# Block products for the feed-forward of the last two batches, behind attention

## The chip, the cores and the metric

The kernel runs on one core of one Trainium2 chip. The time is device time of one execution in microseconds (us); three runs of the kernel before took 323.27, 323.76 and 324.39 us. The engines are PE (TensorE matmul; its weight loads are shown as PEld), VectorE (DVE), ScalarE (ACT), GpSimd (POOL, which only issues loads here) and SyncE (SP, which issues the stores of the output and the transposing copies of q and k).

## What is computed

Attention over 8 batches, 12 heads, 448 positions, 64 columns per head, with an extra term in the denominator, then a feed-forward over 3584 tokens of 768 columns, with a maximum over three up projections. In float32 in and out:

```python
scores = scale * np.matmul(q, k.transpose(0, 1, 3, 2))
e = np.exp(scores - m)
attn = e / (np.sum(e, axis=-1, keepdims=True) + np.exp(-m) + 1e-09)
x = np.matmul(attn, v)                                  # heads side by side: (3584, 768)
h = np.maximum(np.maximum(x @ w1, x @ w2), x @ w3)      # each (768, 768)
out = h @ w_out                                         # (768, 768)
```

## The kernel before

All matmul operands are float16 in SBUF; sums are float32 in PSUM. Attention is worked in 24 groups of four heads (3 groups make a batch). For one group, `visit` makes seven score tiles (one per 64 keys, line 276), each into a pair of PSUM banks; ScalarE turns each into `eT` with one exponential over 128x896 (line 299); `sum_e` on VectorE adds the seven up in `eS` (line 308); `den_group` multiplies `eS` with ones (line 322), and ScalarE takes the logarithm (line 341) and the exponential of its negative (line 348), which is the reciprocal `rb`; `num_group` makes the seven matmul steps of e times v (`av`, line 322) into another pair of banks, and two `norm_group` on VectorE multiply by `rb` and write `xT` (line 375), the transposed input of the feed-forward.

The feed-forward of a batch is cut in pieces. An up piece is a 128-row block of h for one batch and one of the three weights: six matmul steps of 448 columns. VectorE copies it to `hT` (line 497) or takes the maximum with what is there (line 499). An out piece is 128 output rows by 384 columns (`nh` is 0 or 1): six steps of 384 columns; VectorE scales it to float32 in `o_sb` (line 542), and a row tile of 128 x 768 goes out by two stores of 192 KB each on SP's queue (line 560). `o_sb` has six buffers. A pair of batches has 36 up pieces and 14 out pieces.

The order of PE's work is written by hand. From 73 us on, a "step" is one contraction step of a piece, made of four 64x64 matmuls, two for each half of the contraction rows (`step` and `half_step`; the matmul is line 758). `ORDER` (line 827) lists a group's operations, U (score tile), D (den) and N (av), each with a weight; after each operation `steps_for` puts in a share of feed-forward steps, by that weight over the sum of 38.9. `batch_done` adds a finished batch's pieces and sets `rate`, the steps per group. The four last out pieces of each batch are held back and come first with the next batch's out pieces. Pieces rotate over four PSUM banks (`ring_bank`); score, den and av tiles take two pairs of banks in turn (`double`), one pair at a time. Before that, a first stretch to 73 us has attention of the first groups and full-array feed-forward pieces (lines 510 and 533).

When attention is over, the remaining pieces run one after the other: before the change this is the feed-forward of the last batch and what is left of the one before.

Engines work through their instructions in order. So a matmul whose bank is not free, or whose input is not ready, holds every later matmul.

Of the kernel before, what the change touches and what calls it, by code (L numbers as in the profile page):

```python
# [10 lines left out]
FP32 = mybir.dt.float32  # L11
FP16 = mybir.dt.float16
AF = mybir.ActivationFunctionType
ALU = mybir.AluOpType
# [4 lines left out]
EDIV = 8.0  # L19
# [3 lines left out]
def kernel(  # L23
# [33 lines left out]
    )  # L57

    cpool = ctx.enter_context(tc.tile_pool(name="const", bufs=1))
    ld_pool = ctx.enter_context(tc.tile_pool(name="ld", bufs=5))  # L60
    p16_pool = ctx.enter_context(tc.tile_pool(name="p16", bufs=3))
    att_pool = ctx.enter_context(tc.tile_pool(name="att", bufs=4))
    e_pool = ctx.enter_context(tc.tile_pool(name="e", bufs=3))
    small = ctx.enter_context(tc.tile_pool(name="small", bufs=2))
    xt_pool = ctx.enter_context(tc.tile_pool(name="xt", bufs=2))
    ht_pool = ctx.enter_context(tc.tile_pool(name="ht", bufs=2))
    out_pool = ctx.enter_context(tc.tile_pool(name="outp", bufs=6))

    ps1 = ctx.enter_context(tc.tile_pool(name="ps1", bufs=2, space=bass.MemoryType.PSUM))
    ps2 = ctx.enter_context(tc.tile_pool(name="ps2", bufs=1, space=bass.MemoryType.PSUM))
    third = ExitStack()
    ps3 = third.enter_context(tc.tile_pool(name="ps3", bufs=1, space=bass.MemoryType.PSUM))
    turn = [0]
# [61 lines left out]
            reason="spreads the loads",  # L137
        )

    first_k = cpool.tile([128, 2, NJ, D], FP32, name="first_k")  # L140
    load_half(nc.sync, first_k, "k", 0, 0)
    load_half(nc.scalar, first_k, "k", 0, 1)
    load_group(0, "q")
# [22 lines left out]
                )  # L166
    w_sb = [cpool.tile([128, NDC, DFF], MMDT, name=f"w{i}") for i in range(4)]
    wout_sb = w_sb[3]


    def load_weight(i, f0=0, f1=DFF):
# [65 lines left out]


    def first_group():
        k16 = p16_pool.tile([128, NJ, 2, D], MMDT, tag="k16", name="k16", bufs=1)  # L240
        qkT = att_pool.tile([128, 2, NJ, 128], MMDT, tag="qkT", name="qkT")
        state[0] = {"qkT": qkT}
        cuts = (((0, 4), (0, 3)), ((4, NJ), (3, NJ)))
        for (k0, k1), _ in cuts:
            nc.vector.tensor_copy(
                out=k16[:, k0:k1].rearrange("p j s d -> p s j d"), in_=first_k[:, :, k0:k1]
            )
        for (k0, k1), (q0, q1) in cuts:
            nk = k1 - k0
            trT = single("trT", (NJ, 128), MMDT)  # L250
            for j in range(k0, k1):
                nc.tensor.transpose(
                    out=trT[:, j - k0, :], in_=k16[:, j].rearrange("p s d -> p (s d)"),
                    identity=ident16,
                )
            for j in range(q0, q1):
                transpose_slots(trT[:, nk + j - q0, :], raw[0]["q"][:, :, j])
            nc.vector.tensor_copy(out=qkT[:, 0, k0:k1], in_=trT[:, 0:nk])
            nc.vector.tensor_copy(out=qkT[:, 1, q0:q1], in_=trT[:, nk:NJ])
# [70 lines left out]
    def den_group(i):  # L330
        st = state[i]
        dps = double("den")
        av_tiles(
            [dps[:, r, 0:S] for r in range(2)],
            lambda r, c: ones16[half(r)],
            lambda r, c: st["eS"][half(r), c],
            True,
            True,
        )
        st["lnd"] = small.tile([128, 2, S], FP32, tag="lnd", name="lnd")  # L340
        nc.scalar.activation(  # L341
            out=st["lnd"], in_=dps[:, :, 0:S], func=AF.Ln, bias=1.0 / EDIV
        )

    def recip_group(i):
        st = state[i]
        st["rb"] = small.tile([128, 2, S], FP32, tag="rb", name="rb")
        nc.scalar.activation(  # L348
            out=st["rb"], in_=st.pop("lnd"), func=AF.Exp, bias=math.log(LAMBDA), scale=-1.0
        )  # L350

    def num_group(i, in_pair=True):
# [66 lines left out]
    def den_part(i, part):  # L419
        st = state[i]  # L420
        q0, q1 = PARTS[part]
        nq = (q1 - q0) * KC
        eT = st["eT", part]
        dps = double("den")
        terms = [eT[:, j] for j in range(NJ)]
        if "eP" in st:
            eP, n = st.pop("eP")
            terms = [eP[:, 0], eP[:, 1]] + terms[n:]
        for n, e in enumerate(terms):
            av_tiles(  # L430
                [dps[:, r, 0:nq] for r in range(2)],
                lambda r, c: ones16[half(r)],
                lambda r, c: e[half(r), c],
                n == 0,
                n == len(terms) - 1,
            )
        lnd = small.tile([128, 2, S], FP32, tag="lnd", name="lnd")
        nc.scalar.activation(
            out=lnd[:, :, 0:nq], in_=dps[:, :, 0:nq], func=AF.Ln, bias=1.0 / EDIV
        )  # L440
        rb = small.tile([128, 2, S], FP32, tag="rb", name="rb")
        nc.scalar.activation(
            out=rb[:, :, 0:nq], in_=lnd[:, :, 0:nq], func=AF.Exp, bias=math.log(LAMBDA), scale=-1.0
        )
        st["rb", part] = rb

# [80 lines left out]
    def out_piece(bp, t, nh, bank=None, done=False):  # L527
# [4 lines left out]
        for fc in range(0 if done else NFC):  # L532
# [6 lines left out]
            )  # L539
        last = bp == B // 2 - 1 and t == NT - 1  # L540
        cut = nh * NW + (NW // 2 if last and nh == NH - 1 else NW)
        nc.vector.tensor_scalar(  # L542
            out=o_sb[:, nh * NW : cut],
            in0=op_ps[:, 0 : cut - nh * NW],
            scalar1=1.0 / LAMBDA,
            scalar2=None,
            op0=ALU.mult,
        )
        if cut < nh * NW + NW:
            nc.scalar.activation(  # L550
                out=o_sb[:, cut:DM], in_=op_ps[:, NW // 2 : NW], func=AF.Copy, scale=1.0 / LAMBDA
# [153 lines left out]

    third.close()
    flush()
    single_pools.append(ctx.enter_context(tc.tile_pool(name="ps4", bufs=2, space=bass.MemoryType.PSUM)))
    pair_pools.pop()
    LAG = 2  # L710
    flow = []
# [64 lines left out]
    def left():  # L776
        return NDC * (len(pieces) + len(flow)) - count[0]
# [60 lines left out]
    TOTAL = sum(w for _, _, w in ORDER)  # L838


    def batch_done(b):
        add_ups(b)
        last_batch[0] = b == B - 1
        pieces.extend(held)
        held.clear()
        add_out(b, *((0, 3) if b % 2 == 0 else (3, 7)))
        if b < B - 1:
            held.extend(pieces[-HELD:])
            del pieces[-HELD:]
        rate[0] = (left() - (SPARE if b < B - 2 else LAST)) / 3  # L850

    SPARE, LAST = 30, 50
    rate = [0]
    batch_done(1)
    after(9, sum_e, MID, 1)
    after(14, sum_e, MID, 2)
# [3 lines left out]
    for i in range(MID, NI + 1):  # L860
        for op, j, w in ORDER if i > MID else ORDER[4:]:
            if op == "U" and i < NI:
                mm = visit([(i, j)])
                n, name = ((2, "v"), (3, "k"), (3, "q"), (0, ""))[j // 2]
                if n > 0 and i + n < NI and i > MID:
                    load_behind(mm, i + n, name, j % 2)
                steps[0] += 1
                if j == 2:
                    recip_group(i - 1)
                if j > 0:  # L870
                    after({1: 9, 2: 14, 3: 20, 4: 9, 5: 9, 6: 9}[j], sum_e, i, j)
                if j == (9 if i == 7 else 3) and PE_TR <= i + 2 < NI:
                    for n_ in range(2):
                        copy_qk(i + 2, n_)
                    dma_transpose(i + 2)
# [16 lines left out]
            steps_for(rate[0] * w / TOTAL if i < NI else (8 if op == "D" else 0))  # L892
    while late or left() or count[1] < count[0]:
        step()


# [28 lines left out]
```

## Time and profile before

| | |
|---|---|
| median of three runs | 323.76 us (323.27 to 324.39) |
| span of the profiled execution | 322.9 us, about 0.9 us below the median |
| PE busy | 308.2 us, 95% of the span |
| VectorE busy | 235.3 us, 73% |
| ScalarE busy | 191.7 us, 59% |
| last matmul ends | 317.45 us |
| share of the chain that ended last | PE 79%, DMA 14% |

The chain that ended last is followed back from the last instruction, at each step to what released it. It lies on loads until about 56 us and on PE after that. ScalarE's share is low because it has nothing to do after 274 us, when attention is over; in windows of 30 us before that it is 64 to 71% busy, and VectorE 79 to 80%. The mean of one instruction is its duration; instructions of one engine overlap a little, so that two 128x448 operations of VectorE start 0.53 us apart although each lasts 0.62.

### The profile page before, as it was taken

The numbers are of one execution on the slowest core, as the hardware profiler recorded it, in microseconds if no ns is written. First come the engines' busy times: TensorE is split into PE (matmuls) and PEld (weight loads), VectorE is DVE, ScalarE is ACT, GpSimd is POOL, SyncE is SP. The second block draws the span as 40 slices with busy tenths as digits, with TensorE's granted clock in tenths as the row PEclk, the third lists the DMA queues.
The fourth block names the chain that finished last, engine by engine and source line by source line (L and its number), as shares of the span: only waits on it lengthen the run. The fifth ranks groups of instructions, "written<-read, shape, count | busy, mean of one in ns | idle before, by whom it ended". The sixth has DMA issues, their size and how long they took to land.

```text
span 322.9 us, 14605 instructions
## 1 busy us (share of the span) xinstructions
PE 308.2 (95%) x6607; PEld 260.1 (81%) x6607; DVE 235.3 (73%) x443; ACT 191.7 (59%) x227; POOL 96.8 (30%) x166
## 2 busy tenths in 40 slices
PE   7669998999999999999999999999999999999993
PEld 6557676658998899988889877897787788887892
DVE  3446598998887878777769688878778777645652
ACT  2898859887786565575575685685576674000000
POOL 8947565840433132232222232232220000000000
PEclk9999999999999999999999999999999999999999
DMA  7999999999877975779969997899966500050046
GB/s 143 165 191 186 190 190 188 163 159 185 119 98 105 197 135 94 116 147 163 76 99 150 198 150 111 103 179 157 92 81 124 136 4 2 2 150 2 2 122 175
DMA packets 59517, 40.75 MB, mean 126 GB/s; under 512 B 32704, under 2 KB 56000, under 8 KB 59456
## 3 DMA queue, kind: packets, MB, share of 16 engines
q0 software_dynamic: 25344, 21.01, 48.1%
q1 hardware_dynamic: 33808, 18.39, 28.3%
q8 instruction: 51, 0.84, 1.1%
q10 hardware_dynamic: 304, 0.43, 0.5%
q14 instruction: 10, 0.08, 0.1%
HBM read 42.47 MB, written 11.01 MB: 166 GB/s over the span
## 4 chain that ended last, share of the span: by engine, by line
PE 79%; DMA 14%; POOL 3%; issue 1%; DVE 1%; ACT 0%; ACTq 0%; DVEq 0%; POOLq 0%
PE piece L758 59%; PE av L322 9%; PE stp L276 8%; DMA w<-in_moe_w_dram 7%; DMA ld_q<-in_q_dram 4%; DMA w<-in_moe_w_out_dram 2%; PE piece L533 2%; PE den L322 1%; PE piece L510 1%; DMA out_dram<-o_sb 1%; POOL w L180 1%; POOL w L181 1%; POOL ld_v L111 1%; POOL ld_q L111 1%; DVE eS L308 0%
## 5 line engine op out<-in xcount | busy, mean ns | idle before, releaser
L758 PE MATMUL piece<-xT,w 64*64 64x448 f16 x3024 | 177.7, 349 | 0.3 <-DVE xT L375 0.3
L299 ACT ACTIVATE eT<-stp 128x896 f16<-128x896 f32 x147 | 132.8, 916 | 65.9 <-PE stp L276 63.3
L758 PEld LDWEIGHTS <-w 64*64 64x64 f16 x3024 | 132.1, 107 | 21.2 <-issue 1.6
L276 PE MATMUL stp<-qkT 64*64 64x448 f16 (+2 forms) x756 | 71.3, 331 | 2.4 <-ACT eTp L394 0.8
L758 PE MATMUL piece<-w,hT 64*64 64x384 f16 x1224 | 68.3, 323 | 0.0
L308 DVE TENSOR_TENSOR eS<-eS,eT 128x896 f16<-128x896 f16 x105 | 65.0, 619 | 2.7 <-DVE eS L308 0.5
L499 DVE TENSOR_TENSOR hT<-hT,piece 128x448 f16<-128x448 f16 x84 | 51.9, 618 | 19.8 <-PE piece L758 16.8
L758 PEld LDWEIGHTS <-hT 64*64 64x64 f16 x1224 | 53.6, 107 | 4.4 <-issue 0.7
L111 POOL DMA_DIRECT2D ld_q<-in_q_dram x48 | 28.9, 606 | 60.3 <-PE piece L758 33.9
L111 POOL DMA_DIRECT2D ld_v<-in_v_dram x48 | 28.5, 599 | 47.7 <-PE stp L276 30.1
L276 PEld LDWEIGHTS <-qkT 64*64 64x64 f16 x756 | 32.1, 106 | 10.2 <-issue 5.5
L542 DVE TENSOR_SCALAR o_sb<-piece 128x384 f32<-128x384 f32 (+1 forms) x56 | 29.7, 550 | 13.4 <-PE piece L758 12.8
L497 DVE CAST hT<-piece 128x448 f16<-128x448 f32 x42 | 26.1, 621 | 14.4 <-PE piece L758 13.8
L111 POOL DMA_DIRECT2D ld_k<-in_k_dram x46 | 27.7, 609 | 27.5 <-PE piece L758 12.0
L322 PE MATMUL av<-eT,ld_v 64*64 64x448 f16 x588 | 33.3, 349 | 0.0
L322 PEld LDWEIGHTS <-ld_v 64*64 64x64 f16 x756 | 28.7, 107 | 4.2 <-issue 0.2
L375 DVE TENSOR_TENSOR xT<-av,rb 128x448 f16<-128x448 f32 x42 | 24.3, 619 | 9.0 <-PE av L322 8.8
L550 ACT ACTIVATE o_sb<-piece 128x192 f32<-128x192 f32 x1 | 0.3, 330 | 44.6 <-DMA out_dram<-o_sb 44.6
L510 PEld LDWEIGHTS <-w 128*128 128x128 f16 x216 | 18.8, 98 | 6.2 <-issue 4.1
L341 ACT ACTIVATE lnd<-den 128x896 f32<-128x896 f32 x21 | 19.3, 917 | 7.2 <-PE den L322 6.6
L394 ACT ACTIVATE eTp<-stp 128x768 f16<-128x768 f32 (+3 forms) x24 | 18.0, 821 | 7.1 <-PE stp L276 7.1
L348 ACT ACTIVATE rb<-lnd 128x896 f32<-128x896 f32 x21 | 20.0, 951 | 0.2
(50 smaller groups left out, 158.0 us busy)
## 6 DMA issues: line engine op xcount, KB each, us to landing
out_dram<-o_sb SPq DMA_DIRECT2D x54, 192.0 KB, 4.0
ld_q<-in_q_dram POOLq DMA_DIRECT2D x48, 112.0 KB, 4.3
ld_v<-in_v_dram POOLq DMA_DIRECT2D x48, 112.0 KB, 3.8
ld_k<-in_k_dram POOLq DMA_DIRECT2D x46, 112.0 KB, 4.2
w<-in_moe_w_dram POOLq DMA_DIRECT2D x6, 192.0 KB, 6.7
w<-in_moe_w_out_dram POOLq DMA_DIRECT2D x3, 384.0 KB, 7.6
w<-in_moe_w_dram POOLq DMA_DIRECT2D x2, 384.0 KB, 6.2
w<-in_moe_w_dram POOLq DMA_DIRECT2D x1, 576.0 KB, 8.3
```

Source lines behind the costliest of these rows:

```text
L111: return eng.dma_start(out=dst[hp * KC : hp * KC + KC].rearrange("p s j d -> p s (j d)"), in_=src[:, half_heads(name, hp)],)
L276: mm = nc.tensor.matmul(out=out[half(c), r], lhsT=qkT[half(r), 0, j, h], rhs=qkT[half(r), 1, q0:q1, h], start=True, stop=True,)
L299: nc.scalar.activation(out=st["eT"][:, j], in_=stp[:, :, 0:S], func=AF.Exp, scale=scale, bias=-math.log(EDIV))
L308: nc.vector.tensor_tensor(out=st["eS"], in0=st["eT"][:, 0] if j == 1 else st["eS"], in1=st["eT"][:, j], op=ALU.add,)
L322: nc.tensor.matmul(out=outs[r][half(c)], lhsT=weights(r, c), rhs=moving(r, c), start=start, stop=stop,)
L348: nc.scalar.activation(out=st["rb"], in_=st.pop("lnd"), func=AF.Exp, bias=math.log(LAMBDA), scale=-1.0)
L375: nc.vector.tensor_tensor(out=xT[b][:, 2 * g + r, :], in0=banks[r][:, 0:S], in1=state[i]["rb"][:, r], op=ALU.mult)
L497: nc.vector.tensor_copy(out=dst, in_=p_i[:, 0:S])
L499: nc.vector.tensor_tensor(out=dst, in0=dst, in1=p_i[:, 0:S], op=ALU.max)
L510: nc.tensor.matmul(out=p_i[:, ts(j, nq)], lhsT=w_sb[i][:, dc, ts(2 * fp + j, 128)], rhs=xT[b][:, dc, q0 * KC : q1 * KC], start=(dc == 0), ...
L542: nc.vector.tensor_scalar(out=o_sb[:, nh * NW : cut], in0=op_ps[:, 0 : cut - nh * NW], scalar1=1.0 / LAMBDA, scalar2=None, op0=ALU.mult,)
L758: nc.tensor.matmul(out=p["bank"][half(c), 0:w], lhsT=lhs(k, r, c), rhs=rhs(k, r), start=(r == p["first"] and k == 0), stop=(r != p["first" ...
```

## The change

The feed-forward of batches 6 and 7 (`LATE` and the one after it) is taken out of the interleaving with attention. During attention only batches 0 to 5 are worked in pieces, spread evenly over the groups that remain (`batch_done` computes `rate` anew), and 30 steps and the four held out pieces are left for the end.

Behind attention, the two batches are worked as 2 x 2 block products in Winograd's form of Strassen's scheme: seven block products instead of eight, with sums of blocks. For up, the rows of x are split by batch, the contraction and the columns of the weight into halves of 384. For each weight, four combinations of weight blocks (`combine_weight`, 128x1152 float16 subtracts) and, once, four combinations of x blocks (`combine_moving`, 128x1344) are made on VectorE; weight 0's and one x combination already in the last two attention groups. One unit (`up_unit`) is 128 rows of a weight's two halves for both batches: products p1 to p7 of three full-array matmuls of 448 columns each, into two PSUM banks `a` and `s`, several of them accumulated on top of an earlier product. ScalarE copies four results per unit out of PSUM, VectorE makes three sums of a copy and a bank, and for weights 1 and 2 one maximum over 128x1792 (`largest`). Three units run in turn, product by product. For the output, 768 of the 896 rows are worked the same way in three units (`out_unit`, products of three matmuls of 384 columns; two units in turn, then the third together with the plain last row tile). Each unit ends with p4 and p3, after which two row tiles are stored. Four plain out pieces stand between up and out.

Besides: out pieces with `nh == 1` are scaled by ScalarE instead of VectorE, except in the last row tile; `o_sb` has five buffers instead of six; `xT` has three instead of two; the logarithm and the reciprocal share one tile `rb`; `first_k` and `k16` use buffers of `qk16`; the pools of attention are released before the tail, and the tail has all eight PSUM banks.

```diff
-    out_pool = ctx.enter_context(tc.tile_pool(name="outp", bufs=6))
+    out_pool = ctx.enter_context(tc.tile_pool(name="outp", bufs=5))
...
-        st["lnd"] = small.tile([128, 2, S], FP32, tag="lnd", name="lnd")
+        st["rb"] = small.tile([128, 2, S], FP32, tag="rb", name="rb")
         nc.scalar.activation(
-            out=st["lnd"], in_=dps[:, :, 0:S], func=AF.Ln, bias=1.0 / EDIV
+            out=st["rb"], in_=dps[:, :, 0:S], func=AF.Ln, bias=1.0 / EDIV
         )
...
+        if nh == 0 or last:
+            nc.vector.tensor_scalar(
+                out=o_sb[:, nh * NW : cut],
+                in0=op_ps[:, 0 : cut - nh * NW],
+                scalar1=1.0 / LAMBDA,
+                scalar2=None,
+                op0=ALU.mult,
+            )
+        else:
+            nc.scalar.activation(
+                out=o_sb[:, NW:DM], in_=op_ps[:, 0:NW], func=AF.Copy, scale=1.0 / LAMBDA
+            )
...
     def batch_done(b):
-        add_ups(b)
-        last_batch[0] = b == B - 1
+        if b < LATE:
+            add_ups(b)
+            last_batch[0] = b == LATE - 1
...
-        rate[0] = (left() - (SPARE if b < B - 2 else LAST)) / 3
+        coming = sum(NFC * 3 + (6 if x % 2 == 0 else 8) for x in range(b + 1, LATE))
+        steps_left = left() + NDC * (coming + (len(held) if b < LATE - 1 else 0))
+        rate[0] = (steps_left - LAST) / max(NI - max(3 * b + 3, MID) - 0.4, 1)
...
+    def combine_weight(i, n):
+        w, t, m = w_sb[i], comb[i], DFF // 2
+        b11, b12 = w[:, 0:3, 0:m], w[:, 0:3, m:DFF]
+        b21, b22 = w[:, 3:6, 0:m], w[:, 3:6, m:DFF]
+        in0, in1 = ((b12, b11), (b22, t[:, 0]), (b22, b12), (b21, t[:, 1]))[n]
+        nc.vector.tensor_tensor(out=t[:, n], in0=in0, in1=in1, op=ALU.subtract)
...
+                if i == NI - 2 and j in (1, 3, 4, 6):
+                    after(4, combine_weight, 0, (1, 3, 4, 6).index(j))
+                if i == NI - 1 and j == 5:
+                    after(4, lambda: combine_moving(sx, 2, *x_blocks()))
...
+    tps = ctx.enter_context(tc.tile_pool(name="tps", bufs=8, space=bass.MemoryType.PSUM))
+    for n in (0, 1, 3):
+        sx[n] = tail.tile([128, 3, S], MMDT, name=f"sx{n}")
+        combine_moving(sx, n, *x_blocks())
...
+        def p1():
+            bank_of(u, "a")
+            copy("p1", product(u, "a", lambda k: w[:, k, c0], lambda k: x1[:, k], S, True))
+        def p2():
+            bank_of(u, "s")
+            bank = product(u, "s", lambda k: w[:, 3 + k, c0], lambda k: x1[:, 3 + k], S, True)
+            put(0, 0, bank, u["p1"])
+        def p6():
+            copy("u2", product(u, "a", lambda k: t[:, 1, k, c0], lambda k: sx[1][:, k], S, False))
+        def p7():
+            copy("p7", product(u, "s", lambda k: t[:, 2, k, c0], lambda k: sx[2][:, k], S, True))
+        def p5():
+            bank = product(u, "a", lambda k: t[:, 0, k, c0], lambda k: sx[0][:, k], S, False)
+            put(1, 1, bank, u["p7"])
+        def p4():
+            bank = product(u, "s", lambda k: t[:, 3, k, c0], lambda k: x2[:, 3 + k], S, False)
+            put(1, 0, bank, u["u2"])
+        def p3():
+            bank = product(u, "a", lambda k: w[:, 3 + k, c1], lambda k: sx[3][:, k], S, False)
+            put(0, 1, bank)
...
+        if i == 0:
+            return [p1, p2, p7, p6, p5, p4, p3]
+        return [p1, p2, p6, p7, p5, p4, p3, largest]
...
+    for i in range(3):
+        in_turn([up_unit(i, f) for f in range(3)], later(i + 1))
+    for x in [x for f, a, w in held for x in plain(*a)]:
+        x()
+    h_blocks = hp[:, 0:3, 0:NT3], hp[:, 3:6, 0:NT3], hp[:, 0:3, NT3 : 2 * NT3], hp[:, 3:6, NT3 : 2 * NT3]
+    for n in range(4):
+        sh[n] = tail.tile([128, 3, NT3], MMDT, name=f"sh{n}")
+        combine_moving(sh, n, *h_blocks)
+    in_turn([out_unit(0), out_unit(1)])
+    a = out_unit(2)
+    b = plain(B // 2 - 1, NT - 1, 0) + plain(B // 2 - 1, NT - 1, 1)
+    for x in (a[0], b[0], a[1], a[2], b[1], a[3], a[4], b[2], a[5], a[6], b[3]):
+        x()
```

## The prediction

> **What bounds the kernel now.** I read four views: the page's slices, busy time by window, the chain of waits, and the timeline around PE's few pauses. First the slices and windows (columns of a window: PE, PEld, DVE, ACT and POOL busy, granted clock, DMA share, GB/s).
>
> ```profile
> span 322.9 us, 14605 instructions
> PE   7669998999999999999999999999999999999993
> PEclk9999999999999999999999999999999999999999
> 62.00:73.00 11.00, 10.60 (x186) 5.85 (x186) 10.74 (x22) 9.87 (x12) 5.23 (x9) 1.00 1.15 161
> 180.00:210.00 30.00, 29.98 (x644) 24.21 (x638) 24.04 (x46) 19.31 (x23) 8.73 (x16) 1.00 0.92 132
> 210.00:240.00 30.00, 30.00 (x648) 24.40 (x642) 23.98 (x45) 19.71 (x23) 8.77 (x15) 1.00 0.94 132
> 240.00:270.00 30.00, 29.83 (x654) 24.50 (x650) 23.96 (x45) 21.32 (x25) 0.00 (x0) 1.00 0.34 74
> ```
>
> From 73 us PE hardly pauses, at full clock, while VectorE is 80% and ScalarE 64 to 71% busy. So matmul time counts one for one, if nobody keeps PE waiting. What a matmul costs is read from the chain and timeline (start, length, what, how many):
>
> ```profile
> 172.42 1.79 PE piece L758 x44
> 265.68 1.70 PE piece L758 x36
> 63.88 2.11 PE L533 MATMUL piece<-w,hT 128*128 128x384 f16 x12
> 74.90 1.32 PE av L322 x28
> 273.44 1.32 PE av L322 x28
> ```
>
> Four 64x64 matmuls do a full one's work: 1.79/11 = 0.163 us per four of 384 columns, 1.70/9 = 0.189 of 448. Full-array matmuls of 384 columns: (2.11 - 0.33 of the last one)/11 = 0.162. Both forms run at one speed. The two `av` lines bound 17 groups: 198.5/17 = 11.68 us each.
>
> Then PE's margins:
>
> ```profile
> 249.52 0.62 DVE L308 TENSOR_TENSOR eS<-eS,eT 128x896 f16<-128x896 f16 x1
> 250.19 0.38 PE L322 MATMUL den<-eS,ones 64*64 64x448 f16 x4 [0.17 <-DVE eS L308]
> 184.05 1.15 DVE L375 TENSOR_TENSOR xT<-av,rb 128x448 f16<-128x448 f32 x2
> 185.25 0.38 PE L276 MATMUL stp<-qkT 64*64 64x448 f16 x4
> ```
>
> `den` starts 0.05 us after the last sum; a score starts 0.05 us after the second norm freed its pair of banks. Such margins are already used up in some groups. Last, the end:
>
> ```profile
> 314.76 2.34 DMA out_dram<-o_sb
> 317.10 0.56 DVE o_sb L542
> 312.00:314.00 2.00, 2.00 (x57) 2.00 (x52) 0.68 (x2) 0.00 (x0) 0.00 (x0) 1.00 0.78 199
> 318.00:320.00 2.00, 0.00 (x0) 0.00 (x0) 0.00 (x0) 0.33 (x1) 0.00 (x0) 1.00 0.88 215
> ```
>
> PE's last matmul ends at 317.45; the last eviction waits for a store to free its tile, and stores run to about 322. Behind PE lie 5.4 us.
>
> **The change part by part.** The sum is made against the span, 322.9 us; the median, 323.76, is 0.9 above it, which is launch and end around the span.
>
> *Matmuls.* Up: 3 weights x 3 units x 7 products x 3 = 189 full matmuls for 216 fours; 27 x 0.189 = 5.1 us. Down: 63 for 72; 9 x 0.163 = 1.5. **-6.6.** Where rows of weights load before each matmul, the 30 L533 matmuls show loads of 0.098 us that leave the spacing at 0.162, so the loads cost nothing.
>
> A rule speaks against this: the Trainium skill, "TensorE: Matmul & The Clock Gate", Part 3, says that a weight load overlaps running matmuls only where the row group differs. A full-array load would then never hide; by that rule the 288 full matmuls would pay an estimated 0.1 us each, +28 us. The L533 rows contradict it and decide.
>
> *Middle, 62 to 73 us.* Two of its evictions (0.37 us on ScalarE, the spacing of its 384-column activations) join a ScalarE that is busy 9.87 of 11 us and hands scores back to PE. Between 0 and 2 x 0.48 (whole durations): **+0.8**, nearer the top since this engine has 10% left.
>
> *Attention, shorter groups.* Behind the last `av` there are now 24 steps of 0.163, 189 x 0.189 and (63 + 36) x 0.163, together 55.8 us; before, 317.45 - 274.76 = 42.7. So 13.1 + 6.6 = 19.7 us of matmuls leave the 17 groups, 1.16 us each; a group falls to 10.5 us with the same attention work. `den` follows the group's last score by 13 of the order's 38.9 shares, so it loses 0.39 us of margin; the score that reuses `av`'s pair follows it by 10.2 shares and loses 0.30. In the trace, 13 `den` started 0.06 to 1.16 us after their sum (0.06, 0.14, 0.16, 0.34, 0.44, ...); what exceeds the margin sums to 1.2 us. The same for 13 scores after norms (0.05, 0.06, 0.47, ...): 0.65. Scores after exponentials: about 0.3. VectorE gets lighter by 16 evictions of 0.47, but also gets five subtracts of about 0.75 in the last two groups. Bounds: 0, and 17 x 0.69 = 11.7. **+2.2**, by the measured margins.
>
> *Attention, evictions on ScalarE.* About 16 (half of 33 pieces). ScalarE works in order. Around `den` it has exp, Ln, exp, reciprocal back to back: 0.80 + 0.81 + 0.80 + 0.84 = 3.25 us of 10.5, 31% of the time. An eviction that falls there waits 1.6 on average; its bank is one of four in a ring, and matmuls of a later piece queue behind it on PE. Evictions today leave a median 0.45 us before their bank is wanted, and a second free bank gives about 0.5 more. 0.31 x (1.6 - 0.95) = 0.2 each. Bounds: 0 and 16 x 0.8 (one exponential each). **+3.2.** SP's stores now wait for ScalarE too; behind them stand the transposes of q and k, needed two groups (21 us) later, which hides it. The in-place Ln waits for a norm two groups back; first_k and k16 use buffers that are free until group 8: nothing.
>
> *Into the tail.* The first product waits until the last two pieces have left their banks: between 0 and 0.6 (one eviction), **+0.5**.
>
> *Tail, up.* VectorE makes three dependent subtracts over 1344 elements. Its f16 rows space at 0.53 us per 896 and 0.60 per 1024, so 0.78, plus the 0.1 that dependent L499 pairs show: 2.65 us, then the first block sum, before PE's seventh product, 18 x 0.189 = 3.4 us on, may reuse that bank: +0.5. After that a block of three units costs PE 63 x 0.189 = 11.9; VectorE 9 sums x 0.57, 4 subtracts x 0.7 and 3 maxima x 1.04 = 11.0; ScalarE 12 copies x 0.42 = 5.0. Nothing is added while that order holds.
>
> *Tail, down.* After the last up product VectorE still has three maxima (3.1), two evictions (0.95) and four subtracts (2.9), 7 us; PE's cover is 24 plain matmuls and 12 of the first products, 5.85. **+1.0** there. At the end a `o_sb` tile (five instead of six) is reused before its store has landed, and ScalarE, which issues one of the last stores itself, queues a copy behind it: **+0.7**. With the 0.5 above, tail +2.2; bounds 0.5 (only the subtract chain) and 6 (VectorE's durations of 0.62 and gaps of 0.1 in full).
>
> *End.* The stores of six row tiles plus one, 14 x 192 KB = 2.75 MB, start only when units 0 and 1 have their p4 sums: 39 matmuls (6.3 us) and 0.7 of waiting before PE's end, less 0.9 for the sums. At the 199 to 215 GB/s of the windows shown they take 13 to 14 us, at 250 GB/s (the best stretch of the same stores, 286 to 288 us: 246) 11. They end 6 to 8 us after PE, for 4.5 before: between +1.5 and +3.5, **+2.4**.
>
> Sum: -6.6 + 0.8 + 2.2 + 3.2 + 0.5 + 2.2 + 2.4 = **+4.7 us**; span 327.6, time 328.4.
>
> **The rivals.**
> *A, faster: the engines keep up.* VectorE sheds 16 evictions, so attention and tail wait for nobody: the terms 2.2, 3.2 and 1.7 of the tail go. -6.6 + 0.8 + 0.5 + 0.5 + 2.4 = -2.4: 321.4. For it: 0.8 us of PE idle in all of 73 to 317 us, and the load of the shorter group (VectorE 0.80 x 11.68 - 0.55 for a piece less - 0.5 for an eviction = 8.3 of 10.5 us; ScalarE 0.66 x 11.68 + 0.4 = 8.1) is below what 73 to 97 us bear without a gap (20.49 and 19.58 of 24). Against it: margins of 0.05 us. It decides once those waits total under 1.9 us; from 1.9 to 3.9 the time is the same.
> *B, VectorE bounds the tail.* Its sums wait for two engines; at 0.62 plus 0.1 gap each, a block takes 9 x 0.72 + 4 x 0.78 + 3 x 1.2 = 13.2 against PE's 11.9: +3.9 over three blocks, 332.3. For it: 92% load by the kind reckoning. Against: no other engine touches these rows then.
> *C, full-array products do not reach the speed of fours over long stretches.* Every 0.01 us costs 2.9; 0.02 gives 334. L533 speaks against it.
>
> **How the numbers follow.** Forecast (slower by 1 to 2%) 0.63, B 0.14, C 0.04, A 0.12, and 0.07 for a sum in between that ends within 0.3%, about what a measurement of this kernel can tell from no change. Slower is 0.63 + 0.14 + 0.04 = 0.81. The range 322.8 to 332.3 leaves out A's case and what lies beyond B; where it is slower, 325.5 to 331.
>
> **What would show it.** Right: PE's windows between 75 and 255 us show 0.2 to 1.2 us idle per 30, ended by VectorE sums, norms and ScalarE evictions; the first full-array block product starts near 264; PE ends near 318.5; 6.5 to 8 us follow it; full matmuls space at 0.189. Wrong: PE without gaps up to the tail (A), PE waiting for VectorE in every block of three units (B), or spacing above 0.2 (C). Most uncertain is the price of an eviction on ScalarE, which is only reckoned.

## The result, and the profile after

After the change the kernel takes 328.67 us, the median of four runs (327.57 to 329.42); before, beside it on the same chip, 324.07 (323.27 to 324.80). The ratio is 1.0134, with an interval of 1.0091 to 1.0176: 2.9 to 5.7 us slower. The prediction had 328.4 and "slower". One run in this document, 335.75 us of the kernel with 60 more steps behind attention, was a slow execution at a lower granted clock (0.982) and is left out of that kernel's median.

The profiled execution of after is the fastest of its four: 327.57 us with a span of 325.4. These two lines are from its page (the slices of the second are tenths of the granted clock):

```profile
span 325.4 us, 12708 instructions
PEclk9999999999999999999999999999999999999998
```

1897 instructions fewer, the clock is full until PE is done, and still the span is longer. The windows say where (columns as before: PE, PEld, DVE, ACT, POOL busy, granted clock, DMA share, GB/s):

```profile
165.00:195.00 30.00, 28.70 (x620) 23.79 (x614) 23.25 (x44) 22.41 (x29) 9.76 (x17) 1.00 0.87 158
195.00:225.00 30.00, 29.00 (x624) 22.14 (x619) 24.16 (x46) 22.74 (x28) 10.06 (x18) 1.00 0.87 125
225.00:255.00 30.00, 29.60 (x621) 21.88 (x615) 25.78 (x47) 23.04 (x27) 0.56 (x1) 1.00 0.28 54
277.00:289.00 12.00, 12.00 (x65) 6.17 (x64) 7.95 (x15) 6.61 (x13) 0.00 (x0) 1.00 0.00 0
289.00:301.00 12.00, 12.00 (x65) 6.26 (x64) 10.80 (x18) 6.59 (x13) 0.00 (x0) 1.00 0.01 1
301.00:309.00 8.00, 7.35 (x46) 4.22 (x44) 7.60 (x11) 3.33 (x8) 0.00 (x0) 1.00 0.36 98
```

During attention PE now idles 0.1 to 1.3 us in a window of 30 (0.4 to 1.3 in the three shown), where before it idled at most 0.2. While the block products of up run, to 301 us, it does not idle at all; at the hand-over to the output (301 to 309 us) it does, and there VectorE is busy 7.60 of 8 us. The group list of PE between 75 and 264 us names who ended the pauses:

```profile
L766 PE MATMUL piece<-xT,w 64*64 64x448 f16 x2128 | 132.6, 349 | 1.4 <-ACT o_sb L552 0.9 <-DVE hT L498 0.2
L766 PE MATMUL piece<-w,hT 64*64 64x384 f16 x792 | 50.0, 323 | 0.6 <-DVE hT L500 0.6
L279 PE MATMUL stp<-qkT 64*64 64x448 f16 x460 | 47.9, 350 | 1.0 <-DVE xT L377 1.0
L325 PE MATMUL den<-eS,ones 64*64 64x448 f16 x68 | 7.1, 361 | 0.7 <-DVE eS L311 0.6
```

Idle time in this view is smaller than the time lost, since the last matmul's own latency of 0.35 us counts as busy. The loss itself comes from start times. Three of them are in the timeline of after, the first step of the interleaved stretch and two of the pauses in full; the last matmul and the first stores behind it are the last lines:

```profile
72.08 1.28 PE L766 MATMUL piece<-xT,w 64*64 64x448 f16 x16 [0.40 <-DVE xT L377]
...
182.09 0.92 ACT L344 ACTIVATE rb<-den 128x896 f32<-128x896 f32 x1
182.90 0.91 ACT L302 ACTIVATE eT<-stp 128x896 f16<-128x896 f32 x1
183.70 0.95 ACT L350 ACTIVATE rb<-rb 128x896 f32<-128x896 f32 x1
184.54 0.49 ACT L552 ACTIVATE o_sb<-piece 128x384 f32<-128x384 f32 x1
185.08 0.57 PE L766 MATMUL piece<-xT,w 64*64 64x448 f16 x8 [0.92 <-ACT o_sb L552]
...
264.81 1.86 PE L958 MATMUL bank_a<-xT,w 128*128 128x448 f16 x9 [0.58 <-ACT o_sb L552]
...
317.72 0.65 PE L1101 MATMUL bank_a<-w,hT 128*128 128x384 f16 x3
318.37 3.30 SPq L1032 DMA_DIRECT2D out_dram<-o_sb  x4
```

The lines from 182.09 to 185.08 are what the prediction was most afraid of: an eviction on ScalarE stands behind logarithm, exponential and reciprocal, and PE waits 0.92 us for its bank.

To compare runs, I cut each trace at three points: the start of the first 64x64 step, the start of the first block product, and the end of the last matmul. From each length I subtract the column time of its matmuls (0.189 us for four of 448 columns or one full, 0.163 for 384; unrounded 0.1892, from the 188 spacings between 264.81 and 300.37 us in after, and 0.1625). What is left is time that PE lost. The start before the first step differs by up to 3 us from run to run (72.07 to 75.03 us in the profiled runs) and is left out.

| us | first step | attention, length - columns = lost | tail, lost | behind PE's end |
|---|---|---|---|---|
| before | 72.86 | 244.59 - 241.73 = 2.86 (to PE's end, with its tail) | | 5.42 |
| after | 72.08 | 192.72 - 183.32 = 9.40 | 53.56 - 51.84 = 1.72 | 7.06 |

So after the first step the matmuls give 241.73 - 183.32 - 51.84 = 6.6 us, attention loses 6.5 more, the tail 1.7, and the end is 1.6 longer: +3.3. The middle stretch, from one and the same full-array matmul (at 60.09 us before, 58.49 after) to the first step, was 12.77 us and is 13.59: +0.8. Together +4.1 us of the measured +4.6, whose interval is 2.9 to 5.7.

### The profile page after: what moved, and what is told of

The parts are those of the page before. It is cut to its first block, busy times and chain, and to the rows that moved or that the text cites. A ratio compares the mean times of both kernels' runs of the same rounds, so it can differ in the third digit from the quotient of the medians.

```text
span 325.4 us, 12708 instructions
## 1 busy us (share of the span) xinstructions
PE 305.0 (94%) x5599; PEld 226.4 (70%) x5599; DVE 240.8 (74%) x440; ACT 224.9 (69%) x296; POOL 97.1 (30%) x166
## 5 line engine op out<-in xcount | busy, mean ns | idle before, releaser
L766 PE MATMUL piece<-xT,w 64*64 64x448 f16 x2160 | 134.8, 349 | 1.8 <-ACT o_sb L552 0.9
L766 PEld LDWEIGHTS <-w 64*64 64x64 f16 x2160 | 87.3, 107 | 22.1 <-issue 4.2
L766 PE MATMUL piece<-w,hT 64*64 64x384 f16 x792 | 50.0, 323 | 0.6 <-DVE hT L500 0.6
L500 DVE TENSOR_TENSOR hT<-hT,piece 128x448 f16<-128x448 f16 x60 | 37.1, 619 | 15.3 <-PE piece L766 13.7
L766 PEld LDWEIGHTS <-hT 64*64 64x64 f16 x792 | 34.8, 107 | 5.5 <-issue 1.0
L112 POOL DMA_DIRECT2D ld_k<-in_k_dram x46 | 27.9, 610 | 23.6 <-PE piece L766 10.5
L344 ACT ACTIVATE rb<-den 128x896 f32<-128x896 f32 x21 | 19.3, 919 | 4.8 <-PE den L325 3.5
L498 DVE CAST hT<-piece 128x448 f16<-128x448 f32 x30 | 18.6, 620 | 2.3 <-PE piece L766 2.2
L350 ACT ACTIVATE rb<-rb 128x896 f32<-128x896 f32 x21 | 20.0, 954 | 0.2
L544 DVE TENSOR_SCALAR o_sb<-piece 128x384 f32<-128x384 f32 x19 | 10.6, 555 | 11.7 <-PE piece L766 9.8
L958 PEld LDWEIGHTS <-comb 128*128 128x128 f16 x108 | 10.6, 98 | 9.9
```

Source lines behind the costliest of these rows:

```text
L112: return eng.dma_start(out=dst[hp * KC : hp * KC + KC].rearrange("p s j d -> p s (j d)"), in_=src[:, half_heads(name, hp)],)
L344: nc.scalar.activation(out=st["rb"], in_=dps[:, :, 0:S], func=AF.Ln, bias=1.0 / EDIV)
L350: nc.scalar.activation(out=st["rb"], in_=st["rb"], func=AF.Exp, bias=math.log(LAMBDA), scale=-1.0)
L498: nc.vector.tensor_copy(out=dst, in_=p_i[:, 0:S])
L500: nc.vector.tensor_tensor(out=dst, in0=dst, in1=p_i[:, 0:S], op=ALU.max)
L766: nc.tensor.matmul(out=p["bank"][half(c), 0:w], lhsT=lhs(k, r, c), rhs=rhs(k, r), start=(r == p["first"] and k == 0), stop=(r != p["first" ...
```

## The experiments

All times are medians, beside runs of the kernel before on the same chip (323.96 to 324.23 us); a ratio has its interval. The table gives the same cuts for all, each from one profiled execution. Three kernels have the same code in attention and show how far to trust a difference there: after loses 9.40 us, the two with half stores alone 10.04 and 9.37. So less than 0.7 us between two such numbers says little by itself. The expectations speak of pauses of 7.3 us in attention for the changed kernel, a smaller count than the 9.40 of the table.

| us | lost in attention | lost in the tail | behind PE's end | time | ratio |
|---|---|---|---|---|---|
| before | 2.86 | | 5.42 | 324.07 | 1 |
| after | 9.40 | 1.72 | 7.06 | 328.67 | 1.0134 |
| before, evictions on ScalarE | 4.20 | | 5.40 | 325.75 | 1.0051 (1.0030 to 1.0072) |
| after, evictions on VectorE | 9.01 | 2.66 | 7.10 | 328.06 | 1.0130 (1.0094 to 1.0165) |
| eight plain products | 8.03 | 0.16 | 4.87 | 329.39 | 1.0157 (1.0118 to 1.0195) |
| earlier sums | 7.59 | 1.74 | 6.75 | 327.13 | 1.0084 (1.0054 to 1.0114) |
| no combined operands | 8.02 | 0.89 | 7.15 | 326.14 | 1.0063 (1.0036 to 1.0090) |
| 60 more steps behind | 12.18 | 1.75 | 6.82 | 331.47 | 1.0216 (1.0181 to 1.0252) |
| half stores, GpSimd's queue | 10.04 | 1.62 | 8.41 | 329.63 | 1.0170 (1.0135 to 1.0205) |
| half stores, ScalarE's queue | 9.37 | 4.87 | 5.08 | 329.63 | 1.0171 (1.0125 to 1.0218) |
| VectorE evictions and earlier sums | 6.70 | 2.68 | 7.34 | 326.32 | 1.0064 (1.0037 to 1.0090) |
| these, new order in the tail, half stores on GpSimd's queue | 6.30 | 0.18 | 9.73 | 325.35 | 1.0046 (1.0023 to 1.0069) |
| the same with GpSimd only for the first six | 6.27 | 0.17 | 7.30 | 323.21 | 0.9967 (0.9942 to 0.9993) |

### One part alone: ScalarE evictions in the kernel before

```diff
         cut = nh * NW + (NW // 2 if last and nh == NH - 1 else NW)
-        nc.vector.tensor_scalar(
-            out=o_sb[:, nh * NW : cut],
...
-        )
+        if nh == 0 or last:
+            nc.vector.tensor_scalar(
+                out=o_sb[:, nh * NW : cut],
...
+            )
+        else:
+            nc.scalar.activation(
+                out=o_sb[:, NW:DM], in_=op_ps[:, 0:NW], func=AF.Copy, scale=1.0 / LAMBDA
+            )
```

> The kernel before with one part of the change alone: out pieces with nh == 1 are scaled by ScalarE instead of VectorE, except in the last row tile (27 evictions). My theory, that such an eviction waits behind exp, Ln, exp and reciprocal on ScalarE and then holds a PSUM bank that PE wants: 0.8 us in the middle stretch and 0.05 to 0.2 us for each of 25 others (groups are longer here, so margins are wider), 2 to 5 us slower than before, with new pauses of PE ended by ScalarE's line of the eviction. The rival, that ring of four banks hides an eviction on any engine: within 0.5 us of before.

It took 325.75 us for 323.96: +1.8, below my price and above the rival's. Two groups of PE in this kernel between 75 and 264 us:

```profile
L763 PE MATMUL piece<-xT,w 64*64 64x448 f16 x2296 | 141.3, 350 | 0.8 <-ACT o_sb L551 0.8
L763 PE MATMUL piece<-w,hT 64*64 64x384 f16 x792 | 49.8, 323 | 0.3 <-ACT o_sb L551 0.2
```

The middle stretch grows by the 0.8 us that I had reckoned (12.77 to 13.59). In attention only a few evictions make PE wait; the others are early enough. There 1.3 us more are lost, 0.05 for each of 25 evictions, a quarter of the 0.2 that the prediction has.

### The same part taken back: VectorE evictions in the kernel after

```diff
-        if nh == 0 or last:
+        if True:
             nc.vector.tensor_scalar(
```

> The changed kernel with that one part undone: every out piece scaled by VectorE. My theory prices the evictions on ScalarE at 3.2 + 0.8 us, so 2 to 4 us faster than the changed kernel (about 325 to 327 us), if VectorE bears 16 more evictions of 0.47 us. The rival, that PE's pauses in the shorter groups come from VectorE being late with sums and norms, whoever evicts: within 0.7 us of the changed kernel, as what ScalarE gives back VectorE takes.

The kernel took 328.06 us, 0.6 less by the medians, and 1.0130 for 1.0134 as a ratio: nothing is won that can be measured. In its trace no eviction on ScalarE ends a pause any more, but evictions on VectorE do in their place. These are groups of PE from 250 us to its end:

```profile
L766 PE MATMUL piece<-w,hT 64*64 64x384 f16 x192 | 10.3, 324 | 0.8 <-DVE o_sb L544 0.6 <-DVE hT L500 0.2
L958 PE MATMUL bank_a<-xT,w 128*128 128x448 f16 x27 | 5.6, 353 | 0.8 <-DVE o_sb L544 0.8
```

Attention loses 0.4 us less, the tail 0.9 more. Set beside after matmul by matmul, the trace shows where. The middle stretch is 0.8 us shorter again (12.78), and at 255 us this kernel is another 1.35 us ahead, most of it by the pause at 185 us that is gone. But 0.96 of that goes at the hand-over to the block products (PE idles 0.56 and 0.78 us behind evictions on VectorE) and another 0.9 at the one to the output. So the evictions on ScalarE cost time, but moving all of them back gives most of it away at the two hand-overs; a split by place was not tried.

### The placement without the block products

The same pieces are left behind attention, but computed as eight plain products with full-array matmuls; the combinations, sums and copies are gone.

```diff
-                if i == NI - 2 and j in (1, 3, 4, 6):
-                    after(4, combine_weight, 0, (1, 3, 4, 6).index(j))
-                if i == NI - 1 and j == 5:
-                    after(4, lambda: combine_moving(sx, 2, *x_blocks()))
...
+    for b in (LATE, LATE + 1):
+        for fc in range(NFC):
+            for i in range(3):
+                full(up_piece, b, fc, i)
+        if b == LATE:
+            for f, a, w in held:
+                full(f, *a)
+    for t in range(NT):
+        for nh in range(NH):
+            full(out_piece, LATE // 2, t, nh)
```

> The changed kernel with the feed-forward of the last two batches at the same place behind attention, in full-array matmuls, but as plain pieces: eight block products, no block sums on VectorE, row tiles stored as they come. My theory (shorter attention groups cost 6.7 us with the middle stretch and the hand-over, the tail's sums 2.2, the late stores 2.4, seven for eight products give 6.6): 6.6 - 2.2 - 2.4 = 2 us slower than the changed kernel, 330 to 331 us, with PE's pauses before 264 us as in the changed kernel and none after. The rival, that attention costs nothing and the tail's sums and stores eat the gain: 324 to 325 us, as before the change.

It took 329.39 us (ratio 1.0157). With the column time of before, no block sums and a shorter end than before (4.87), it is still 5.4 us slower, and nearly all of that time stands in attention: 8.03 us lost for 2.86. Moving the work out of attention is what costs, together with the evictions on ScalarE and the changed buffers, which this kernel has too; the buffers were not tried alone. The seven products for eight save 6.6 us behind it and give 5.1 of that back: 1.6 in the tail, 2.2 at the end, 1.4 in attention (9.40 for 8.03). By the medians they are worth 0.7 us where I had expected 2, and since the intervals of the two ratios overlap, not even that is shown by the times.

### More of the same: 60 steps more behind attention

```diff
-LAST = 30
+LAST = 90
```

> The changed kernel with 90 instead of 30 feed-forward steps left behind attention: the same work, but each attention group has 3.6 steps (0.65 us) less between its operations. My theory, that PE's pauses come from groups that are short against fixed delays on VectorE and ScalarE: pauses in attention grow from 7.3 to 9 or 10 us, 1.5 to 3 us slower than the changed kernel. The rival, that pauses belong to fixed places (evictions, bursts of out pieces) whatever the group's length: within 0.7 us.

It took 331.47 us, 2.8 more than after. The matmuls are the same and the tail loses the same; attention loses 12.18 us for 9.40. In the groups of PE between 75 and 264 us the denominators now wait for the sums:

```profile
L325 PE MATMUL den<-eS,ones 64*64 64x448 f16 x68 | 6.8, 366 | 2.6 <-DVE eS L311 1.9 <-ACT eT L302 0.2
```

That is 2.6 us for 0.7 in after and 0.2 before. The change took 19.7 us of matmuls out of attention and lost 6.5; this one took 9.8 to 11.3 more (60 steps of 0.163 to 0.189) and lost 2.8 more. On average each us taken out comes back as 0.25 to 0.33 us of waiting, with the order left as it was; the 0.33 also contains the evictions and the subtracts.

### Earlier sums

The sums of the exponentials are put 2 to 4 steps earlier after their score, so that the denominator finds them done.

```diff
-                    after({1: 9, 2: 14, 3: 20, 4: 9, 5: 9, 6: 9}[j], sum_e, i, j)
+                    after({1: 7, 2: 11, 3: 16, 4: 7, 5: 7, 6: 7}[j], sum_e, i, j)
```

> The changed kernel with the sums of exponentials put earlier into the order: 7, 11, 16, 7 steps after their score tile instead of 9, 14, 20, 9, in proportion to the shorter groups. My theory, that the den matmul waits for the last sum because the group got shorter while the sums' place did not: PE's pauses before den go, 1 to 2 us faster than the changed kernel. The rival, that the pauses come from ScalarE's evictions and from banks: within 0.5 us of the changed kernel.

It took 327.13 us, 1.5 less than after, as expected; attention loses 7.59 us for 9.40. Three groups of PE between 75 and 264 us:

```profile
L766 PE MATMUL piece<-xT,w 64*64 64x448 f16 x2160 | 135.9, 350 | 2.6 <-ACT o_sb L552 0.9 <-DVE hT L500 0.6 <-DVE hT L498 0.5
L279 PE MATMUL stp<-qkT 64*64 64x448 f16 x464 | 50.8, 350 | 0.4 <-DVE xT L377 0.4
L325 PE MATMUL den<-eS,ones 64*64 64x448 f16 x68 | 7.4, 353 | 0.1
```

The denominators' wait is gone (0.7 to 0.1) and the scores wait less for norms (1.0 to 0.4), but pieces now wait for VectorE's maxima (L500, 0.6) and copies (L498, 0.5). The sums had been placed for groups of 11.68 us; at 10.5 the same distance in steps is too late. That is a term of my "shorter groups", and part of it is a setting that the change did not renew.

### Both of these

The edits of the evictions on VectorE and of the earlier sums in one kernel.

> The changed kernel with all evictions on VectorE and the sums of exponentials 7, 11, 16, 7 steps after their scores. Alone, the first gave 0.6 us and the second 1.5. My theory now, that in the short groups a fixed delay on either engine ends the pause and the later of two counts: the two together give more than their sum, 2.5 to 3.5 us faster than the changed kernel, pauses in attention about 4.5 us. The rival, that VectorE's load is the limit and early sums only shift it: 1.5 us or less.

It took 326.32 us, 2.4 less than after, a little under what was expected and about the sum of the two (0.6 + 1.5): that they give more together than alone is not shown. Attention loses 6.70 us, but the tail 2.68 for 1.72: VectorE enters the tail later, as in the kernel with evictions alone.

### Without the combined operands

The block products use plain blocks in place of their combinations. The combinations (all subtracts on VectorE) are left out of the computation, the products, sums and copies are all there.

```diff
-                if i == NI - 2 and j in (1, 3, 4, 6):
-                    after(4, combine_weight, 0, (1, 3, 4, 6).index(j))
-                if i == NI - 1 and j == 5:
-                    after(4, lambda: combine_moving(sx, 2, *x_blocks()))
...
-        combine_moving(sx, n, *x_blocks())
+    for n in range(4):
+        sx[n] = x_blocks()[(3, 2, 0, 1)[n]]
...
-        combine_moving(sh, n, *h_blocks)
+        sh[n] = h_blocks[(3, 2, 0, 1)[n]]
```

> The changed kernel with the combined operands left out: the products take blocks of x, h and the weights as they are, so the 16 weight subtracts, four x and four h combinations on VectorE are not made and the output is not the reference's; products, copies, sums, maxima and stores stay. My theory, that PE's pauses in the tail (1.5 us in the changed kernel's trace) come from VectorE making operands and first sums: 1 to 1.5 us faster than the changed kernel, pauses at the seventh product of the down units gone. The rival, that they come from copies and banks: within 0.4 us.

It took 326.14 us, 2.5 less than after, more than expected. In the tail 0.8 us go. The larger part, 1.4, goes in attention: its loss is 8.02 us, the same as with eight plain products (8.03), which also has no subtracts there. So the five subtracts in the last two groups cost 1.4 us of PE's time. Set beside after matmul by matmul, both of these kernels keep step with it to within 0.1 us up to 240 us and gain the 1.4 between there and the first block product, where the subtracts are. The 0.8 in the tail is gained between 305 and 308 us, at the hand-over to the output. I had named the five subtracts and put no price on them.

### The end: half stores on a second queue

Here the units' tiles go out in stores of half the columns, as soon as a half is ready; every second store is issued on another queue, and the tiles have six buffers of their own. First GpSimd's queue:

```diff
-            nc.sync.dma_start(out=rows[j][:, n0:n1], in_=o[half(n), n0:n1])
+            (nc.sync, nc.gpsimd)[n].dma_start(out=rows[j][:, n0:n1], in_=o[half(n), n0:n1])
...
-            u["o1"] = out_pool.tile([128, DM], FP32, tag="o_sb", name="o_sb")
+            u["o1"] = tail.tile([128, DM], FP32, tag="o_t", name="o_t", bufs=6)
...
+            store(m, u["o1"], 0, NW)
...
+            store(3 + m, u["o2"], NW, DM)
...
-            store(3 + m, u["o2"], 0, DM)
+            store(3 + m, u["o2"], 0, NW)
...
-            store(m, u["o1"], 0, DM)
+            store(m, u["o1"], NW, DM)
```

> The changed kernel with the tail's stores spread: each row tile of a block unit goes out in two column halves as soon as each is summed, the second row half on GpSimd's queue instead of SP's, and the units' output tiles have six buffers of their own. Nothing else changes. My theory, that 7.1 us lie behind PE's last matmul because the units store late and through one queue: 5 to 5.5 us behind it, 1.5 to 2.5 us faster than the changed kernel. The rival, that the bytes themselves (2.75 MB at about 250 GB/s) set the end: within 0.5 us.

It took 329.63 us, and 8.41 us lie behind PE for 7.06. The transfers did come earlier: the last store landed 3.6 us after PE's end, at 323.27 (in after 5.9, at 324.26). But the span runs to 328.1. The end of its chain of waits, and the slices of its transfers from 314 us on (0.4 us each):

```profile
319.53 0.52 POOL out_dram L1032
320.05 0.52 POOLq L1163
```

```profile
GB/s 292 223 230 296 215 292 250 242 311 296 325 315 85 12 180 277 242 292 277 327 330 73 0 0 0 0 0 0 0 0 0 0 0 0 0 0 0 0 0 0
```

Nothing is moved after 323 us. The trace's instruction records show what is left: GpSimd's closing drain (a DRAIN instruction at the end of its program), which ends at 327.34, 6.8 us after its last issue had ended at 320.57. ScalarE's own last drain takes 0.4 us in after. So next the same on ScalarE's queue:

```diff
-    def store(t, o, n0, n1):
+    def store(t, o, n0, n1, other=nc.scalar):
...
-            (nc.sync, nc.gpsimd)[n].dma_start(out=rows[j][:, n0:n1], in_=o[half(n), n0:n1])
+            (nc.sync, other)[n].dma_start(out=rows[j][:, n0:n1], in_=o[half(n), n0:n1])
```

> The changed kernel with the stores of the block units spread as in e6_spread_stores, in column halves as they are summed, but with the second row half on ScalarE's queue instead of GpSimd's, so without GpSimd's drain at the end. My theory, that late stores through one queue cost the end: 5 to 5.5 us behind PE's last matmul, 1 to 2 us faster than the changed kernel. The rival, that issues on ScalarE hold its copies back and PE with them: no gain.

Again 329.63 us. Behind PE there are only 5.08 us, but PE itself loses 4.87 in the tail for 1.72. Two lines of its timeline of PE:

```profile
311.03 1.14 PE L958 MATMUL bank_a<-comb,sh 128*128 128x384 f16 x6 [0.82 <-ACT u L1044]
317.78 0.65 PE L958 MATMUL bank_a<-comb,sh 128*128 128x384 f16 x3 [2.21 <-ACT p L1044]
```

An issue on ScalarE waits for VectorE's sum, and ScalarE's own copies out of PSUM, for which PE waits, stand behind it: from 312.4 to 317.2 us ScalarE issues six stores, 0.5 to 0.8 us each, and makes two evictions before the copy that the second line waits for. The end gets 2 us shorter and the tail 3.1 longer.

### All together, and then with the later stores on ScalarE's queue

Evictions on VectorE, earlier sums, two weights of the order within a group changed, half stores on GpSimd's queue, and the three output units in turn, product by product, with the last row tile's four halves after the second, fourth, fifth and sixth product, instead of two units and then the third:

```diff
-        ("U", 1, 4.5),
+        ("U", 1, 6),
...
-        ("U", 6, 4),
+        ("U", 6, 2.5),
...
-    in_turn([out_unit(0), out_unit(1)])
-    a = out_unit(2)
     b = plain(B // 2 - 1, NT - 1, 0) + plain(B // 2 - 1, NT - 1, 1)
-    for x in (a[0], b[0], a[1], a[2], b[1], a[3], a[4], b[2], a[5], a[6], b[3]):
+    a = [out_unit(m) for m in range(3)]
...
```

> The changed kernel with everything that the runs point to: all evictions of out pieces on VectorE, sums of exponentials 7, 11, 16, 7 steps after their scores, shares of the order moved a little (6 after the second score, 2.5 at a group's end), spread stores, and the three down units in turn with the last row tile's pieces between them. My theory: pauses in attention fall from 7.3 to about 3.5 us, the tail's to 0.5, the end to 5.5 to 6, about 6 us faster than the changed kernel: 322 to 323.5 us, a little under the kernel before. The rival, that what one place gives back another takes: 325 us or more.

It took 325.35 us, 2 to 3 above what was expected, and the cause is again the closing drain: 9.73 us lie behind PE, the last store landed at 321.6, GpSimd's drain ended at 325.0, 6.8 us after its last issue had ended at 318.27. So in the next kernel GpSimd issues only the first six half stores, and ScalarE's queue the later ones:

```diff
-            store(m, u["o1"], 0, NW)
+            store(m, u["o1"], 0, NW, nc.gpsimd)
...
-            store(3 + m, u["o2"], NW, DM)
+            store(3 + m, u["o2"], NW, DM, nc.gpsimd)
```

> e8_all again, but GpSimd's queue issues only the first halves' stores (six, in the first half of the down units), and ScalarE's queue the later ones. In e8_all's trace the last store had landed at 321.6 and the span ended at 325.8, with GpSimd's drain between. My theory, that this drain runs 6.8 us from GpSimd's last DMA issue and was all that kept e8_all slow: 3 us faster than e8_all, 322 to 323 us, under the kernel before. The rival, that the drain has a fixed length after the last store wherever GpSimd's last issue lies: no faster than e8_all.

It took 323.21 us (321.94 to 324.59), 2.1 below the last where 3 were expected, and, at a ratio of 0.9967 (0.9942 to 0.9993), 0.3% faster than before, hardly clear of the noise. The drain now ends at 317.8, 2 us before the last store lands. Windows of this kernel:

```profile
165.00:195.00 30.00, 29.43 (x654) 25.78 (x647) 25.36 (x50) 22.52 (x26) 10.29 (x17) 1.00 0.87 158
195.00:225.00 30.00, 29.50 (x638) 23.76 (x634) 25.09 (x49) 22.65 (x27) 9.56 (x16) 1.00 0.85 141
264.00:300.00 36.00, 36.00 (x194) 18.80 (x193) 28.76 (x46) 18.20 (x34) 0.00 (x0) 1.00 0.03 8
```

The tail loses 0.17 us. Attention still loses 6.27, 3.4 more than before, which no edit here removed, and the end is 1.9 us longer than before's. These two take back 5.3 of the 6.6 us saved. The kernel before got none of these edits, and plain products were not run with them; so this comparison does not show what the block products alone are worth.

## Why the prediction was right, and where its terms were not

The total was right: 328.4 for 328.67, slower, and PE's first block product at 264.81 (predicted "near 264"), its end at 318.37 (318.5), 7.06 us behind it (6.5 to 8). The two points of time also hold a start that happened to be 0.8 us earlier than in the profile of before. The sum came out by luck as well as by working: the largest cost was far too high, another far too low, and a third had no term. Point by point:

- *Its own base.* I took the profiled execution of before to lie 0.9 us under its time. In all later runs, of both kernels, the time is 1.7 to 2.2 us above the span. So 322.9 belongs to an execution of nearly 325 us, about 0.9 above the median, and what lies around it was 0.9 too small. The two cancel: the sum of +4.7 us stands against +4.6 between the medians.
- *Matmuls, -6.6.* Right. The nine matmuls at 264.81 take 1.86 us: less 0.35 of the last one, 1.51 for eight, 0.189 each. The rule that I cited from the Trainium skill, "TensorE: Matmul & The Clock Gate", Part 3, does not hold here: over 277 to 301 us the loads of 128 rows take 12.4 of 24 us and PE does not idle.
- *Middle, +0.8.* Right: +0.8, and the same with these evictions alone in the kernel before.
- *Attention, shorter groups +2.2, evictions on ScalarE +3.2, and into the tail +0.5: 5.9 together.* The loss was 6.5, but this is where the working failed: the step "about 16 evictions at 0.2 each" fell. Taken back, the evictions return 0.4 us of attention, because VectorE's evictions make PE wait in other places. Those that cost on ScalarE were mainly two, with 0.92 us of idle PE at 185 and 0.58 at the first block product, not sixteen by a little. The price for short groups, in turn, was far too low: I had counted only margins of denominators, scores and exponentials that I saw in the trace, not the maxima, copies and evictions of pieces, and no price at all for the five subtracts. Of the 6.5, earlier sums recover 1.8, these with VectorE evictions 2.7, and all that was tried in attention 3.1; 3.4 stay in the best version, and the subtracts, 1.4 when they are taken out of the changed kernel, are still in it. The longest pauses that its trace still has are four, all ended by VectorE: 0.65 us of idle PE before the first block product (an eviction), 0.57 at 166 (a maximum), 0.53 at 240 (a copy) and 0.43 at 208 (a norm); none of them was tried further.
- *Tail, +2.2.* 1.7. The hand-over to down, predicted at 1.0, is one pause of 0.82 at 308.23, which ends with a VectorE sum. The wait near the end for ScalarE, predicted at 0.7, is one of 0.62 at 316.64: a copy stands behind ScalarE's issue of a store. The chain of three subtracts at the start (0.5) is not to be seen. Two timeline lines of after:

```profile
308.23 1.14 PE L958 MATMUL bank_s<-comb,sh 128*128 128x384 f16 x6 [0.65 <-DVE o_sb L1051]
...
316.64 0.65 PE L958 MATMUL bank_s<-comb,hT 128*128 128x384 f16 x3 [0.46 <-ACT p L1044]
```

- *End, +2.4.* +1.6. The stores were late as described. One more wait lay in it that I did not have: SP issues its store after the one at 318.37 only at 319.93, since it waits for a store of `o_sb` from ScalarE's queue, which landed at 319.91. The waits of SP's queue from 315 us on put 1.0 us on it:

```profile
SPq L1032 <- DMA out_dram<-o_sb: 1.0, 1, 1.0
```

The rivals. *A* (the engines keep up) needed waits under 1.9 us; they were 8.2 more than before. *B* (VectorE bounds the tail) is against the windows: 7.95 to 10.80 of 12 us busy, and PE without a gap; it holds only at the hand-over to the output, for 0.8 us. *C* (slower full-array products) is excluded by 0.189. The last kernel gets part of the way to A by another road: it does not show that the engines keep up, only that with an order set for the shorter groups attention and tail lose 3.6 us more than before, where the changed kernel loses 8.3.

## What to carry to other kernels

Where one engine is full and its order is set to the others' delays, work taken away from it is not won one for one: here each us of matmuls that left attention came back, on average, as 0.25 to 0.33 us of waiting, on margins that had been hidden. Price such a move by the margins of every instruction that the engine waits for, and set distances that are counted in steps anew when the stretch gets shorter. The wait with the longest line in a profile need not be the cause of the loss: taking it away moved the pause to another engine.

## What the runs showed of the hardware

- GpSimd's drain at the end of its program ran on for 5.8 to 7.3 us after its last DMA issue had ended, in all thirteen profiled runs, whether that issue was a load (238.9 to 244.7 us before, 225.6 to 232.6 after) or a store. It costs nothing while others still work. Where late stores were on this queue it set the end: 6.8 us after the last issue (320.6 to 327.3, and 318.3 to 325.0), 4.1 and 3.4 us after the last store had landed.
- A store on SP's queue can wait for the landing of a store from another engine's queue of which it needs nothing (319.91 to 319.93, above). What they share is a completion semaphore in the trace's records; that this is the whole cause was not tested.
- In seven of the eleven experiments' profiled runs the granted clock was 0.5 for 3.4 or 6.8 us between 10 and 19 us, and in four of them the first step started later than in any other run (74.3 to 75.0 us; 72.1 to 73.3 in the other three). The code up to there is the same as in kernels without it, so the edits are an unlikely cause, but it is one reason why a single span is compared here from the first step on.
